# An order planned while the program is built, replaced by one written out in full (two H3 convolution and MLP layers)

## The chip, the cores and the metric

The kernel runs on one core of a Trainium2 chip. The metric is the device time of one execution in microseconds, lower is better. The engines are PE (TensorE, matrix products), DVE (VectorE), ACT (ScalarE), POOL (GpSimd) and SP (SyncE, which here only issues DMAs). Each engine takes its instructions in the order in which they stand in its own queue; an instruction that waits holds up those behind it.

## What is computed

```python
def _A_ref(q, k, v, shift_k, ssm_k, ssm_D):       # B=1, S=2048, D=512, 4 taps
    k_pad = jnp.pad(k, ((0, 0), (ks - 1, 0), (0, 0)))
    for t in range(ks):
        k_shift = k_shift + k_pad[:, t:t + S, :] * shift_k[:, ks - 1 - t][None, None, :]
    kv = k_shift * v
    ...                                            # y: causal convolution of kv with ssm_k
    y = y + kv * ssm_D[None, None, :]              # along S, per channel, by FFT of length 2S
    return q * y

def _B_ref(x, w1, b1, w2, b2):                     # 512 -> 1376 -> 512
    y = _layernorm(x, axis=-1)
    h = _gelu(jnp.einsum("bsd,df->bsf", y, w1) + b1)
    return jnp.einsum("bsf,fd->bsd", h, w2) + b2

x = A_q
x = x + _A_ref(_layernorm(x), A_k, A_v, A_shift_k, A_ssm_k, A_ssm_D)
x = x + _B_ref(_layernorm(x), B_w1, B_b1, B_w2, B_b2)
# the last two lines once more
```

All tensors are bf16. The convolution of `kv` does not depend on `x`, so the kernel computes `y` once and both layers use it.

## The kernel before

**The stages.** The program runs in two parts.

The first part makes `y`. The convolution is a product of spectra, and the transforms are matrix products. For the filter: transposes on PE (tag `ht`, L749), a first transform stage (`h1`, L766, 16 tiles), a second stage (`h2`, L779, 16 tiles), and 16 DMAs that store a copy of the spectrum with its two halves swapped. For `kv`: the four-tap shift of `k` and the product with `v` (tags `fir0` to `fir3`), where channels 0 to 255 go over PE (L810 transposes, L827 products with scaled identities that POOL makes at L741, L834 product with `v` on DVE) and channels 256 to 511 over DVE alone (L658, eight operations of 128x2048 for each 128 channels); then the first stage (`x1`, L766, 16 tiles), the second stage (`x2`, L872, 16 tiles) and the product with the filter's spectrum on DVE (L658, 16 operations), the first inverse stage (`i1`, L896, 16 tiles) and the second inverse stage (`i2`, L953, 10 tiles). The `x2`, `i1` and `i2` tiles come in two halves of the channels, `_0` and `_64`.

Every PE tile of this part goes to a pair of PSUM banks, and is then copied to SBUF by an evacuation, which can be on ACT (L663) or on DVE (L664); a tile whose bank pair is still in use waits for the evacuation of the tile before it there.

The second part runs the layers in blocks of rows (128 rows are a slice; layer 1 has blocks of 1, 1, 2, 2, 2, 2, 2, 2, 2 slices, layer 2 four of 4). Each block has statistics on DVE (L985, L987) with an inverse square root on POOL (L991, L993), a norm (tag `q`, L1000), the product with `y` and the sum into `x` (tag `y`, L658), the statistics and norm once more (tag `z`), and a transpose of the normed slice. That transpose is on PE for the first two slices (L1047) and a DMA on the SP queue for all others (L1039 in the code, two or four of them for a block). Then come the first product of the MLP (`m1`, L1060, 11 tiles of 4 matmuls for a block), GELU on ACT (L1065), the second product (`m2`, L1093, 11 matmuls for a slice) and its sum into `x` on DVE (L1097). The last slice of layer 2 has its second product in three pieces of 256, 128 and 128 columns (L1082, L1086). The results leave by DMAs of 128 or 256 KB, the last ones smaller. Blocks are named z0 to z8 (layer 1) and z19 to z22 (layer 2) after their tags.

**What sets the order.** The program is recorded first: each `P.op(...)` appends an operation with what it reads and writes, and `Prog` derives which earlier operations it depends on. Operations are numbered in the order of recording, 0 to 1113, and both kernels record the same ones under the same numbers. Then `schedule()` (L320 on) simulates the engines with assumed durations: at each step it picks, among the operations that are ready, the one of least start time and highest priority. The priority is the longest way to the end plus offsets from four tables (`BIAS` by tag, `PB` by operation, and delays `SHY`, `PS` and `HOLD`). It also picks the engine where two are allowed, unless the table `ENG` fixes it, and the PSUM banks, from pools: pairs of banks for the first part, and for the MLP one group of at most 3 banks for `m1` and one of at most 3 for `m2`. The engines' queues are the result. `sync()` then puts in the semaphore waits that the dependencies need, and `emit()` writes the instructions.

All loads and DMA transposes stand on the SP queue, but four small loads and one store that stand on ACT's. POOL's queue waits for its own instruction before, each time.

Of the kernel before, what the change touches and what calls it, by code (L numbers as in the profile page):

```python
# [7 lines left out]
ALU = mybir.AluOpType  # L8
# [14 lines left out]
class Pool:  # L23


    def __init__(self, nb, cap, gate=False):
        self.nb, self.cap, self.used, self.gate = nb, cap, 0, gate


class Tile:  # L30


    def __init__(self, pool):
        self.pool = pool
        self.base = None
        self.left = 0
        self.ops = []


class Op:  # L40
    __slots__ = ("i", "engs", "eng", "fn", "dur", "preds", "succ", "prio", "tile", "dma", "start", "end",
                 "pos", "inc", "waits", "val", "npred", "ready", "bytes", "base", "extra", "gate", "tag", "allow")


class Prog:
# [5 lines left out]
    LAT = 155.0  # L51
    BIAS = {'': 1044190, 'fir0': 816272, 'fir1': 594035, 'fir2': 1000293455, 'fir3': 475782, 'h1': 868926, 'h2': 42492, 'ht': 880650, 'i1_0': 1240071, 'i1_64':
        1212024, 'i2_0': 1097582, 'i2_64': 1190749, 'm1': 1032413, 'm2': -1808312, 'q0': 602778, 'q1': 1095651, 'q19': 267875, 'q2': 1096365, 'q20':
        912832, 'q21': 583017, 'q22': 318772, 'q3': 998981448, 'q4': 986060, 'q5': 466064, 'q6': 470208, 'q7': 409268, 'q8': 641212, 'taps': 736508,
        'warm0': 1000949769, 'x1_0': 1331587, 'x1_1': 783401, 'x1_2': 1063685, 'x1_3': 949292, 'x2_0': 377017, 'x2_64': 955361, 'y0': 1650539, 'y1':
        1623078, 'y19': 2204116, 'y2': 1000018107, 'y20': 947043, 'y21': 1812233, 'y22': 1073869, 'y3': 1411221, 'y4': 607830, 'y5': 295728, 'y6':
        405240, 'y7': 620020, 'y8': 1895488, 'z0': 999281074, 'z1': 1641796, 'z19': 1050878, 'z2': 131483, 'z20': -312548, 'z21': 457235, 'z22':
        577125, 'z3': -403715, 'z4': 81537, 'z5': 198870, 'z6': -330710, 'z7': 181103, 'z8': 1650154}
    SHY = {'fir0': 1021, 'fir1': 277, 'h1': 55, 'h2': 0, 'ht': 0, 'i1_0': 0, 'i1_64': 365, 'i2_0': 61, 'i2_64': 0, 'x1_0': 0, 'x1_1': 8, 'x1_2': 1351, 'x1_3':
        1268, 'x2_0': 0, 'x2_64': 462, 'z0': 261, 'z1': 833}  # L60
    PB = {0: 150814, 1: -52106, 2: -225577, 3: -123331, 4: 999221868, 9: 1276405, 44: 1379512, 45: 1434690, 47: 506509, 49: 453148, 51: 999588645, 52:
        1000042154, 53: 1589169, 54: 1589469, 55: 1517533, 56: 1595021, 57: 1561543, 58: 1589849, 59: 1505754, 60: 1589135, 61: 1539763, 63:
        999477473, 64: 999472326, 65: 81483, 66: 1000044663, 67: 999459987, 68: 19356, 69: 999454615, 70: 999472376, 71: -54290, 72: 999450473, 73:
        999474703, 75: 999467239, 76: -144374, 77: 999428971, 78: 239791, 79: 999491599, 80: 245756, 81: 999824582, 82: 168731, 83: 999955057, 84:
        -153184, 85: 1000209098, 86: 182551, 87: 999183272, 88: 316431, 89: 999956485, 90: -132325, 91: 999955107, 92: 228777, 93: 999458556, 94:
        -263977, 95: 1000286130, 96: -155038, 97: 999951289, 98: 491335, 99: 999392283, 100: 370445, 101: 999956535, 102: 370055, 103: 999943327, 104:
        316481, 105: 1000160828, 106: 1184366, 107: 1000314641, 108: 1291204, 109: 1000854551, 110: 1266991, 111: 1000849866, 112: 1230810, 113:
        1262509, 114: 1184316, 115: 745385, 116: 899745, 117: 1262559, 118: 909647, 119: 1001022447, 120: 893995, 121: 1000704463, 122: 834188, 123:
        874451, 124: 883372, 125: 1000706919, 126: 774582, 127: 998790820, 128: 785190, 129: 1000706969, 130: 861289, 131: 998997835, 132: 820442,
        133: 998980303, 134: 656521, 135: 998997885, 136: 907870, 137: 998958853, 155: -39187, 156: -120533, 157: -28284, 158: -97856, 159: 55705,  # L70
        161: -516310, 162: -336038, 163: -518892, 164: 205143, 165: 997729962, 166: -214054, 167: -532152, 169: 999878049, 170: 26055, 171: 341414,
        172: 302525, 173: -46374, 175: -516143, 176: -99172, 177: 431557, 178: -1035368, 179: 998060916, 180: -4231, 181: 998061019, 183: -127374,
        184: -999854529, 185: -1000132297, 186: -999488136, 187: -999485498, 188: -999373078, 189: -999483119, 191: 998075025, 192: -336655, 193:
        997785394, 194: -134666, 195: 998021352, 196: -685036, 197: 997910445, 199: -108657, 200: -207937, 201: 409421, 202: 73116, 203: -307100, 204:
        373599, 205: 669605, 207: 810393, 208: -569320, 209: 792122, 210: 501734, 211: 186163, 212: -176342, 213: 377429, 215: 1000696642, 216:
        998595356, 217: -50, 218: 1275751, 219: 756681, 220: -627082, 221: 998743003, 222: 555542, 223: 45, 224: 75226, 225: -102355, 226: 504322,
        227: 998924854, 228: 759137, 229: -343831, 230: 1363941, 231: 557998, 232: -624626, 233: 1513102, 234: 1001678, 235: 494654, 236: 998659113,
        237: 68724, 239: 639399, 240: -142796, 241: 322586, 242: 192764, 243: 740845, 244: 126297, 245: -566055, 246: 219170, 247: 608048, 248:
        -35318, 249: 380427, 250: 126247, 251: -1127529, 252: 103746, 253: 230758, 255: 998347921, 256: 998431917, 257: -11025, 258: 509829, 259:
        998025019, 260: 366769, 261: 998226716, 262: 998431967, 263: 31, 264: 703634, 265: 998431924, 266: 467759, 267: 922821, 268: 998451943, 269:  # L80
        412967, 270: 998227330, 271: 998451993, 272: 327804, 273: 742271, 274: 998037985, 275: 50337, 276: 999968359, 277: 998434335, 279: 298049,
        280: 152190, 281: 358015, 282: -341491, 283: 417985, 284: -1150, 285: 412598, 286: 226932, 287: -987359, 288: -107162, 289: 350905, 290:
        150350, 291: 634586, 292: -120566, 293: 998096146, 308: 1465845, 309: 1509084, 310: 1454263, 311: 1446566, 312: 1227621, 314: 524321, 315:
        31603, 316: 508933, 317: -181697, 318: 219814, 319: -282525, 320: 998097678, 321: -119423, 322: 485782, 324: 998069011, 325: -235296, 326:
        997992307, 327: -478329, 328: -1033996, 329: -376661, 330: -1029693, 331: -368979, 332: -703260, 334: 998659676, 335: 1899604, 336: 1936265,
        337: 493047, 339: 23181, 340: 997383373, 341: 997684387, 343: -246654, 344: 435848, 345: -996672795, 346: -996548852, 347: 406757, 348:
        -998727435, 349: 188797, 350: -772376, 351: -1657, 352: -560052, 353: 998190809, 354: -90796, 355: -101769, 356: -294390, 357: -22717, 358:
        -187974, 359: 817, 360: -210463, 361: -13499, 362: -297738, 363: 998339095, 364: -856719, 365: 46341, 366: -856722, 367: 47421, 368: -1031847,
        369: 387, 370: -465710, 371: -7105, 372: 1888330, 373: 1889303, 374: 2164277, 375: 2831282, 377: 998090342, 378: 1490839, 379: 1272509, 380:
        998131015, 382: 997525207, 383: 997659852, 384: 997906873, 386: -178, 387: 997432687, 388: 1099648, 389: 729514, 390: 998078479, 391: -667124,  # L90
        392: 997909179, 393: -90181, 395: -287849, 396: -1105208, 397: -643666, 398: 998193901, 399: -716417, 401: -716948, 402: -6378, 403: -1043716,
        404: 998714183, 405: -559050, 406: 998340752, 407: -668160, 408: 48098, 409: -735263, 410: -5564, 411: -296218, 412: 998197275, 413: -639571,
        414: 998616267, 415: 2069863, 416: 1900008, 417: 1873327, 418: 2950942, 420: 525435, 421: 997886742, 422: 526337, 423: 1432173, 424: 1606857,
        425: 597541, 427: -556199, 428: -385679, 429: -639224, 430: 998185257, 431: -467907, 432: -439130, 433: -560982, 434: -386814, 435: 999236624,
        436: 998821254, 437: 937285, 438: 999432304, 439: 999476812, 440: 999488740, 441: 2546841, 442: 2522318, 443: 998831934, 445: 1042685, 447:
# [166 lines left out]
    def op(self, eng, fn, dur, reads=(), writes=(), tile=None, dma=None, prio=0.0, nbytes=0, gate=()):  # L262
        o = Op()
# [10 lines left out]
        for t in o.tile:  # L274
            for p in t.ops:
                preds.add((p.i, "psum"))
# [857 lines left out]
```

## Time and profile before

| | |
|---|---|
| median of 3 runs | 241.92 us (241.72 to 242.06) |
| span of the profiled execution | 239.8 us |
| PE matmul busy | 226.5 us, 94% |
| PE weight loads | 151.5 us |
| DVE busy | 175.7 us, 73% |
| ACT busy | 142.9 us, 60% |
| POOL busy | 34.8 us |
| granted TensorE clock | 1.000 |
| HBM read, written | 16.82 MB, 2.10 MB |

The profiled execution's own time is its span of 239.8 us, from its first to its last instruction, and some 2.1 us around it that the runs' times contain and the span does not. The largest groups of instructions are:

| line, engine | what | count | busy us | mean ns |
|---|---|---|---|---|
| L1060 PE | first MLP product | 568 | 83.7 | 296 |
| L1093 PE | second MLP product | 329 | 78.9 | 379 |
| L663 ACT | evacuations | 79 | 73.9 | 1055 |
| L1065 ACT | GELU | 143 | 67.8 | 522 |
| L658 DVE | shift, spectral products, `y` | 108 | 63.8 | 628 |
| L985 DVE | statistics | 68 | 42.6 | 650 |
| L1000 DVE | norms | 64 | 24.1 | 401 |
| L1097 DVE | sums of the second product | 31 | 20.8 | 682 |

Means count overlap: a DVE or ACT instruction starts before the one ahead of it is done, so its cost on a full engine is the distance from start to start, which is some 0.1 us less than the mean of the large ones. The same holds for matmuls.

### The profile page before, as it was taken

How to read it: one execution, taken by the hardware profiler on the slowest of the kernel's cores; microseconds unless marked ns; L12 is line 12 of the kernel's file. 1: busy time of each engine (PE TensorE's matmuls, PEld its weight loads, DVE VectorE, ACT ScalarE, POOL GpSimd, SP SyncE). 2: the span in 40 equal slices, each digit the busy share in tenths (PEclk: the TensorE clock that was granted, in tenths of full speed). 3: DMA queues.
4: the chain of work that ended last, by engine and by line, in shares of the span. 5: the costliest groups of instructions: out<-in, count | busy, mean ns of one | idle time of the engine just before them, and what ended most of it. 6: DMA issues, size and time to landing. Idle time of an engine off the chain costs nothing.

```text
span 239.8 us, 5559 instructions
## 1 busy us (share of the span) xinstructions
PE 226.5 (94%) x2310; PEld 151.5 (63%) x2330; DVE 175.7 (73%) x363; ACT 142.9 (60%) x223; POOL 34.8 (15%) x75
## 2 busy tenths in 40 slices
PE   7988899886899999999999999999999999999996
PEld 3876777775899885777767665754444444444453
DVE  0779999999997989989999996978997401211214
ACT  3697999999998994665556253464532552436200
POOL 3250000000012222223141032022130100000000
PEclk9999999999999999999999999999999999999999
DMA  6999999999910004222020203313022203210022
GB/s 231 338 387 385 384 235 272 249 282 337 375 63 0 3 0 48 45 44 48 0 44 5 42 1 68 66 23 68 0 44 44 87 3 69 62 44 0 3 98 77
DMA packets 37035, 27.40 MB, mean 114 GB/s; under 512 B 19506, under 2 KB 29969, under 8 KB 37010
## 3 DMA queue, kind: packets, MB, share of 16 engines
q1 hardware_dynamic: 36446, 26.91, 38.1%
q8 instruction: 18, 0.29, 0.5%
q10 hardware_dynamic: 564, 0.14, 0.4%
q14 instruction: 7, 0.06, 0.1%
HBM read 16.82 MB, written 2.10 MB: 79 GB/s over the span
## 4 chain that ended last, share of the span: by engine, by line
PE 71%; DVE 15%; DMA 4%; ACT 4%; SPq 3%; issue 2%; DVEq 0%
PE ps L1060 32%; PE ps L1093 30%; DVE ar L658 8%; PE ps L896 5%; DMA ar<-in_A_v_dram 4%; ACT ar L663 4%; DVE ar L664 4%; SPq L647 3%; DVE ar L834 2%; PE ps L1082 1%; PE ps L872 1%; DVE sm L985 1%; PE ps L953 1%; DVE ar L1000 0%; PE ps L766 0%
## 5 line engine op out<-in xcount | busy, mean ns | idle before, releaser
L1065 ACT ACTIVATE ar<-ps,sm 128x256 bf16<-128x256 f32 (+5 forms) x143 | 67.8, 522 | 72.8 <-PE ps L1060 70.1
L1060 PE MATMUL ps<-ar 128*128 128x256 bf16 (+5 forms) x568 | 83.7, 296 | 0.2
L1093 PE MATMUL ps<-ar 128*128 128x512 bf16 (+1 forms) x329 | 78.9, 379 | 0.7
L663 ACT ACTIVATE ar<-ps 128x1024 bf16<-128x1024 f32 (+2 forms) x79 | 73.9, 1055 | 8.0 <-PE ps L766 3.2
L1060 PEld LDWEIGHTS ps<-ar 128*128 128x128 bf16 (+1 forms) x572 | 53.2, 100 | 29.4 <-ACT ar L1065 0.4
L658 DVE TENSOR_TENSOR ar<-ar 128x512 bf16<-128x512 bf16 (+3 forms) x108 | 63.8, 628 | 1.8 <-DMA ar<-in_A_k_dram 1.4
L1093 PEld LDWEIGHTS ps<-ar 128*128 128x128 bf16 (+1 forms) x341 | 33.2, 98 | 34.5
L1097 DVE TENSOR_TENSOR ar<-ar,ps 128x512 bf16<-128x512 bf16 x31 | 20.8, 682 | 43.2 <-PE ps L1093 43.1
L985 DVE BATCH_NORM_STATS2 sm<-ar 128x6 f32<-128x512 bf16 (+1 forms) x68 | 42.6, 650 | 0.3
L1000 DVE TENSOR_SCALAR ar<-ar,sm 128x512 bf16<-128x512 bf16 x64 | 24.1, 401 | 6.6 <-POOL sm L993 6.3
L993 POOL TENSOR_TENSOR sm<-sm 128x2 f32<-128x2 f32 (+2 forms) x26 | 20.5, 787 | 2.2
L766 PE MATMUL ps<-ar 128*64 128x128 bf16 x512 | 17.6, 221 | 3.0 <-DVE ar L664 1.0
L991 POOL TENSOR_SCALAR sm<-sm 128x2 f32<-128x2 f32 (+2 forms) x26 | 5.9, 226 | 95.9 <-DVE sm L987 95.7
L766 PEld LDWEIGHTS ps<-ar 128*64 128x64 bf16 x512 | 14.9, 110 | 5.4 <-DVE ar L664 1.3
L664 DVE CAST ar<-ps 128x1024 bf16<-128x1024 f32 (+1 forms) x15 | 17.5, 1181 | 0.4 <-PE ps L872 0.2
L896 PE MATMUL ps<-ar 128*128 128x128 bf16 x256 | 15.1, 220 | 1.0 <-DVE ar L658 0.5
L896 PEld LDWEIGHTS ps<-ar 128*128 128x128 bf16 x256 | 14.5, 114 | 1.4 <-ACT ar L663 0.8
L872 PE MATMUL ps<-ar 128*128 128x64 bf16 x256 | 9.6, 193 | 2.3 <-ACT ar L663 2.1
L664 DVE COPY ar<-ps 128x2048 bf16<-128x2048 bf16 (+1 forms) x6 | 5.7, 954 | 7.6 <-PE ps L749 7.4
L987 DVE BATCH_NORM_AGGREGATE sm<-sm 128x2 f32<-128x6 f32 (+1 forms) x64 | 10.8, 177 | 0.6
L872 PEld LDWEIGHTS ps<-ar 128*128 128x128 bf16 x256 | 8.2, 98 | 3.5 <-ACT ar L663 3.4
L779 PE MATMUL ps<-ar 128*128 128x128 bf16 x128 | 8.7, 220 | 0.9 <-ACT ar L663 0.8
(33 smaller groups left out, 72.0 us busy)
## 6 DMA issues: line engine op xcount, KB each, us to landing
ar<-tab_s SPq DMA_DIRECT2D x16, 256.0 KB, 10.0
ar<-ar SPq DMA_DIRECT2D x16, 256.0 KB, 4.6
ar<-in_A_ssm_k_dram SPq DMA_DIRECT2D x4, 512.0 KB, 5.5
ar<-in_A_k_dram SPq DMA_DIRECT2D x8, 256.0 KB, 7.7
ar<-in_A_v_dram SPq DMA_DIRECT2D x8, 256.0 KB, 9.7
ar<-in_A_q_dram SPq DMA_DIRECT2D x4, 512.0 KB, 7.8
out_dram<-ar SPq DMA_DIRECT2D x7, 256.0 KB, 2.0
ar<-in_B_w_dram SPq DMA_DIRECT2D x1, 1376.0 KB, 12.0
```

The source lines that it names most:

```text
L658: return P.op(eng, lambda e: e.tensor_tensor(o, a, b, op), dur, reads=[a, b] + list(more), writes=[o])
L663: return e.activation(dst, src(), AF.Copy)
L664: return e.tensor_copy(dst, src())
L766: r = e.matmul(Q(tl, 64 * ri, 64, i * 128, [1, 128]), w, m, start=True, stop=True)
L896: r = e.matmul(Q(tl, 0, 128, i * 128, [1, 128]), w, m, start=q == 0, stop=q == 1)
L985: P.op(DVE, lambda e, sj=sj, x=x: e.bn_stats(sj, x), 40.0 + 1.1 * w, reads=[x], writes=[sj], gate=gate)
L993: P.op(POOL, lambda e: e.tensor_tensor(r, v, hf, ALU.pow), 430.0 + 150.0 * n, reads=[v, hf], writes=[r])
L1000: P.op(DVE, lambda e: e.tensor_scalar(o, x, m, r, ALU.subtract, ALU.mult), 335.0, reads=[x, m, r], writes=[o])
L1060: r = e.matmul(Q(tl, 0, rows, 0, [1, w]), a, m, start=dk == 0, stop=dk == 3)
L1065: P.op(ACT, lambda e, dst=dst, tl=tl, rows=rows, bias=bias, w=w: e.activation(dst, Q(tl, 0, rows, 0, [1, w]), AF.Gelu_apprx_tanh, bias=bia ...
L1093: r = e.matmul(Q(tl, 0, 128, 0, [1, 512]), ins[fc][0], ins[fc][1], start=fc == 0, stop=fc == 10)
L1097: P.op(DVE, lambda e, x=x, tl=tl: e.tensor_tensor(x, x, Q(tl, 0, 128, 0, [1, 512]), ALU.add), 640.0, reads=[x], writes=[x], tile=tl)
```

## The change

`schedule()`, its tables and the pools go. In their place stand three tables: `ORDER`, one permutation of the numbers 0 to 1113; `SECOND`, the operations that run on the second of their two allowed engines; and `BANKS`, the first PSUM bank of each tile in the order of recording. `arrange()` reads them. The queue of an engine is the subsequence of `ORDER` whose operations are its own. `sync()` and `emit()` stay, but that waits are sorted by place in `ORDER` instead of by simulated end.

```diff
-        self.banks = [(0.0, []) for _ in range(8)]
-        free = {e: 0.0 for e in (PE, ACT, DVE, POOL, SP)}
...
-            k = (s + (self.PS.get(o.i, self.SHY.get(o.tag, 300.0)) if e == DVE and len(o.engs) > 1 and o.dur[DVE] > o.dur.get(ACT, 1e9) else 0.0), -o.prio, o.i)
...
+    def arrange(self):
+        self.order = {e: [] for e in (PE, ACT, DVE, POOL, SP)}
+        last = [None] * 8
+        second = set(self.SECOND)
+        assert sorted(self.ORDER) == list(range(len(self.ops)))
+        for at, i in enumerate(self.ORDER):
+            o = self.ops[i]
+            o.eng = o.engs[i in second]
+            o.at, o.pos = at, len(self.order[o.eng])
+            self.order[o.eng].append(o)
+            tl = o.tile
+            if tl is not None and tl.base is None:
+                tl.base = self.BANKS[tl.i]
+                for b in range(tl.base, tl.base + tl.nb):
+                    if last[b] is not None:
+                        for p in [p for p in last[b].ops if p.eng != PE] or last[b].ops[-1:]:
+                            assert p.eng is not None
+                            if p.i not in o.preds:
+                                o.preds[p.i] = "psum"
+                    last[b] = tl
...
-                    cands.sort(key=lambda x: -x.end)
+                    cands.sort(key=lambda x: -x.at)
...
-            tl = Tile(dconv)
+            tl = Tile(2)
```

`Tile(2)` is a pair of banks, `Tile(1)` a single one (MLP products and the PE transposes of z0 and z1). The tables begin so:

```python
ORDER = (
    0, 47, 8, 7, 48, 5, 3, 71, 68, 72, 73, 6, 1, 62, 98, 104, 16, 2, 69, 4, 65, 15, 63, 70, 64, 53, 102, 11, 13, 32, 49, 57, 99, 66,
    105, 100, 101, 80, 103, 50, 81, 17, 67, 76, 74, 56, 9, 51, 90, 52, 77, 94, 91, 96, 75, 19, 14, 12, 36, 95, 44, 18, 25, 27, 78, 60,
...
SECOND = (
    63, 64, 66, 67, 69, 70, 72, 77, 85, 89, 91, 97, 101, 161, 179, 191, 197, 213, 251, 283, 324, 392)
BANKS = (
    0, 2, 0, 2, 2, 0, 4, 0, 4, 6, 0, 2, 2, 6, 6, 4, 2, 0, 4, 4, 0, 6, 4, 6, 0, 6, 2, 6, 0, 4, 6, 4, 4, 6, 4, 2, 2, 0, 0, 2, 0, 4, 6, 2,
...
```

Put side by side, the two programs differ in this:

- The operations are the same 1114. PE has 343 of them in both, SP 109; ACT has 230 instead of 228, DVE 358 instead of 363, POOL 74 instead of 71.
- 31 operations change engine. From ACT to DVE: one copy of the transposed filter (66), six `h1` evacuations (77, 85, 89, 91, 97, 101), three `x1` (179, 191, 213), two `i1` (251, 283), one `i2` (324). From DVE to ACT: three `h1` (79, 87, 99), three `h2` (113, 117, 123), the copy of the transposed `k` of channels 0 to 127 (155), two `x1` (175, 211), one `x2` (224), three `i1` (249, 285, 293), one `i2` (314), the copy of the transposed slice z0 (349). From DVE to POOL: three additions of `ssm_D` to one row of the filter (64, 67, 70).
- The loads on SP stand in another order: the four filter loads as 8, 7, 5, 6; then `k`, `v` and the 16 loads of the second-stage table mixed, instead of `k`, `v`, table. Each halo load of `k` stands among them (11 early, 10 behind the last of `k`). The swapped copies of the filter's spectrum (138 to 153), the loads of the inverse table (294 to 297), of `A_q` (298 to 301) and of the weights (302 to 307) are mixed too.
- Of the `i2` tiles, 313 now stands before the last four `i1` tiles on PE, and 321 behind the transpose of z0. z0 is transposed before z1, where it was z1 before z0.
- Statistics and norms of later blocks stand earlier on DVE, in part by several blocks. In layer 1, the first two-slice block starts on PE (451) before the second products of the one-slice blocks are done (374, 416, 417 follow).
- On PE the last tile is the 256-column piece of the last slice (1105); it was a 128-column piece (1111).
- 513 of the 624 operations that use a PSUM tile use other banks than before. The number of semaphore waits falls from 976 to 854.

## The prediction

> **What bounds the kernel now.** I read the 40 slices first, then the chain of waits, then the timelines of DVE and ACT, then busy time by stretch.
>
> ```profile
> PE   7988899886899999999999999999999999999996
> DVE  0779999999997989989999996978997401211214
> ACT  3697999999998994665556253464532552436200
> ```
>
> PE is full from about 64 us to the end. Before that DVE and ACT are full (slices 4 to 12), and PE is not. The chain shows the same change of hands:
>
> ```profile
> 63.52 1.13 ACT ar L663
> 64.70 3.84 PE ps L896 x64
> 68.53 0.09 issue
> 68.63 8.21 PE ps L896 x144
> 76.83 0.45 PE ps L953 x4
> 77.31 0.70 DVE ar L664
> 82.61 0.34 DVE ar L1000
> 83.00 0.40 PE ps L1047 x4
> ```
>
> From 64.70 PE works without a gap but at two places: 76.83 to 83.00, where it runs the second inverse stage (L953) level with DVE's first layernorms, and 94.27, where the block after the two one-tile blocks starts 0.04 us after its transposed input landed (94.23).
>
> ```profile
> 200.00:210.00 10.00, 9.95 (x47) 4.50 (x46) 1.97 (x3) 2.74 (x5) 0.00 (x0) 1.00 0.32 74
> 210.00:220.00 10.00, 9.95 (x47) 4.65 (x47) 0.75 (x2) 5.38 (x8) 0.00 (x0) 1.00 0.07 26
> ```
>
> Columns: window, then PE, weight loads, DVE, ACT, POOL, granted clock. PE is at 9.95 of 10 at clock 1.00, and four 128x512 matmuls take 0.86 us, 2.4 columns a ns. Since no matmul is added or removed, the time can only fall by PE idling less before 95 us. So I follow one thing: when PE reaches a given piece of its work. [...]
>
> **The change, part by part.** What fills DVE and ACT:
>
> ```profile
> 16.80 2.36 DVE L658 TENSOR_TENSOR ar<-ar 128x2048 bf16<-128x2048 bf16 x2 [1.43 <-DMA ar<-in_A_k_dram]
> 50.23 18.25 DVE L658 TENSOR_TENSOR ar<-ar 128x2048 bf16<-128x2048 bf16 x16
> 52.62 20.27 ACT L663 ACTIVATE ar<-ps 128x1024 bf16<-128x1024 f32 x22 [0.23 <-DVE ar L658]
> ```
>
> One large DVE operation costs 1.136 us ((18.25-1.21)/15), one ACT evacuation 0.92 (20.27/22; starts are 0.905 apart).
>
> 1. Engines. 13 evacuations go ACT to DVE, 15 DVE to ACT, three 1x128 additions DVE to POOL. DVE's work falls by two evacuations and 0.66 us, about 2.1 us with the small ones (172.2 to 170.1, summed from its row durations); ACT's rises about 1. What matters is where: six of the 16 stage-1 evacuations of the filter and all four of the transposed filter now stand on DVE ahead of the convolution; before it was three and three. Before 16.80, while DVE waits for k (1.43 us), it has done 6 large operations; now it has 9 queued ahead.
>
> 2. Loads. The SP queue lands 256 KB every 0.67 us in order. Two table loads now stand ahead of k's last part and the 0.78 us halo behind it: k lands at 16.78+2x0.67-0.78 = 17.3 instead of 16.78. DVE's nine: first transposed tile at 6.2, 9x1.136+0.2 = 10.4 of work, and about 1.4 of waits, mostly for the fourth filter load (9.73 plus 1.2 of transposes, where DVE was free at 10.1): 18.0. So k's delay is covered by 0.7, and would cost what exceeds that.
>
> 3. Up to the products. Then 25 large DVE operations stand before the first spectral product, 28.4 us: 46.4. Before it was 29 from 16.80, 50.23 with 0.5 idle. ACT agrees: its first stage-1 tile is ready at 9.5 (transposes in step 2, then 0.66 on PE), and ten such evacuations at 0.905, two tap copies of 0.5 and two copies of the transposed k of 1.87 end at 23.3, with small waits 23.5; 24 more at 0.905 bring the first product's tile at 45.2, in SBUF at 46.2; before it was started at 49.53. The 0.43 us of PE per stage-1 tile hides under these. SP's swaps of the filter's halves wait for ACT's evacuation at about 35; the fourth lands near 43, covered by 3; the table loads behind them are first needed at 73.
>
> 4. Products and first inverse. On DVE 17 large operations and one 0.60 bn_stats: 19.9, so the last product ends at 66.5 with 0.2 of waits; before 68.48. PE starts the second half's tiles at 66.95 (before 68.60) and runs eight at 0.89 plus one 0.44 tile of the second inverse, moved between them: 74.5. Before, it ended its last such tile at 76.6 without the 0.44. PE is ahead by 76.6+0.4-74.5 = 2.5.
>
> 5. First layernorms. The moved 0.44 tile and its evacuation on ACT (0.55) let y start at 74.1 instead of 78.03. DVE's queue from there has 5.3 of work to the first z norm and 0.4 of wait: 79.8. PE, with 5.7 of second-inverse tiles after 74.5, transposes that z at 80.3 (before the first at 82.99, with 0.3 lost): ahead by 2.7. Evacuations of the last inverse tiles now sit between ACT's GELUs of the one-tile blocks, 0.26 each: one makes PE wait about 0.15.
>
> 6. Transposed inputs. PE's order puts the first two-tile block 2.2 us of work earlier: ten matmuls of the second MLP product, 0.216 each, now follow its start. From the first z transpose it has 8.8 of work to there (two transposes of 0.22, 0.87 of second inverse, the 22 tiles of the first MLP product at 0.222, 12 matmuls at 0.216), and the gap of 0.3 that it also showed before: 80.3+8.8+0.3 = 89.4. DVE's norms end at 85.2, the two transposes are issued one after the other (1.27 each) and the second lands 2.5 after its issue: 88.8. Before the second took 3.86 (90.37 to 94.23); if that recurs, 90.1, and PE waits 0.7. Counting blocks from z0, I did the same for the later ones: DVE's queue up to the block's last norm, plus its idle so far, plus 3.4 to landing (as for z4 and z5 before), against PE's queue up to the block's first matmul. PE finds each landed, by 0.6 (z3), 0.7 (z5), 1.0 and 0.8 (first two of layer 2) and by over 1 elsewhere; before, this margin was 1.7 to 4 after z2. DVE's longer waits for second-product tiles come behind the norms that are near.
>
> 7. Tail. The last PE tile is 256 wide, not 128: DVE 0.42 for 0.29, landing 1.53 for 1.46: 0.2 lost.
>
> 8. Banks: any of eight instead of two groups of three for the MLP. PE waits for none of them before; the cover is a freed bank 0.7 us ahead, and gone it would cost that wait per block. Nothing, 0 to 0.7.
>
> The three additions on POOL are the one price the trace lacks. Nearest rows: POOL's 128x1 tensor_tensor 0.57, its 128x128 scale 0.61, so 1.2 to 1.8 for three; they delay the eight scaled identities to 18.9, needed by PE at 21.7. Nothing, 0 to 0.3. DVE's 1x128 additions took 0.43 for two while POOL scaled, 0.22 alone, so no stretch. [...]
>
> Sum: 2.7, less 0.2 for ACT, 0.2 for half a late landing and small waits, 0.2 tail: 2.1. Profiled span 239.8, and 2.1 outside it to the median of 241.92; 237.7 + 2.1 = 239.8. Unknowns give 1.2 worse (0.7 landing or banks, 0.3 POOL, 0.2) to 1.1 better (no early waits, 0.9 of the 1.4, and 0.2): 238.7 to 241.0.
>
> **The rivals.**
> - Half of it: the late landing recurs (0.5 more than charged) and bank or POOL waits take 0.5: 240.8. For it: 3.86 was seen once; against: every other pair took 2.4 to 2.6.
> - No change: the early stage is bound by hand-overs. Stage-1 tiles take PE 0.43 start to start but 0.66 start to ready, and in the new order nearly each waits for a bank just freed. With 0.6 instead of 0.43 over some 12 tiles in series the first product comes 2.0 later, 48.5, and the gain is 0.1: 241.8. Against it: before, DVE kept 84% busy through the same stage.
> - Slower: one DVE stall becomes PE's. In the new queue DVE has 30.8 us of work between the first z norm and z5's last norm (before 22.6), since statistics of later blocks are drawn forward. Without idle PE has 0.7 to spare there. Before, DVE idled 3.7 in that stretch (POOL's 0.87 twice among it). If it idles so again, z5's block is 3.0 late, and PE, in order, waits: 239.8+3.0 = 242.8. It decides from 2.8 of idle. Against: the drawn-forward work fills those waits; I find only one of 0.35.
>
> **How the numbers follow.** Forecast 0.52, half 0.20, no change 0.12, slower 0.16. What a measurement can tell is 0.2%, 0.5 us: faster 0.72, same 0.12, slower 0.16. The forecast's own range is 238.7 to 241.0; the range reaches on to 242.4, leaving out most of the slower case and a little below.
>
> **What would show it.** First product on DVE near 46.4; k's wait gone; last product near 66.5; first z transpose on PE near 80.3; the first two-tile block near 89.4; PE then at 9.9 of 10. A first product after 48, or PE idle at a block start above 0.7, proves a step wrong.

## The result, and the profile after

| | before | after |
|---|---|---|
| median, us | 241.95 (241.72 to 242.06, 4 runs) | 244.57 (242.91 to 245.59, 4 runs) |
| ratio after to before | | 1.0103, 95% interval 1.006 to 1.0147 |
| span of the profiled execution, us | 239.8 | 241.1 |
| PE matmul, DVE, ACT busy, us | 226.5, 175.7, 142.9 | 228.3, 172.7, 140.0 |

The changed kernel is 1.0% slower; 239.8 was forecast. The profiled execution after is the fastest of its four (242.91). One execution of the changed kernel in the first experiment below took 598.18 us, and that experiment's figures leave it out.

The slices and the queue of PE's instructions, from the page of the changed kernel:

```profile
PE   6996999887899999999999999999999999999995
DVE  0799699999999999999699789968772532100133
ACT  2397999999999995446426524703584013638000
...
q8 instruction: 18, 0.29, 0.5%
```

As before, PE is full from slice 12 on (66 us); DVE has a 6 in its fifth slice (24 to 30 us), where it had a 9. The stretch that PE bounds has not become shorter or longer (columns as before: window, PE, weight loads, DVE, ACT, POOL, granted clock, DMA share, GB/s):

```profile
200.00:210.00 10.00, 10.00 (x48) 4.51 (x47) 2.06 (x3) 5.46 (x9) 0.00 (x0) 1.00 0.08 28
```

So the loss must stand at the front. The chain of waits after:

```profile
19.62 1.11 PE ps L589 x18
20.74 2.28 issue
23.02 0.94 PE ps L589 x14
23.96 0.89 PE ps L558 x16
24.85 1.76 PE ps L606 x14
26.61 0.02 issue
26.63 1.23 DVE ar L613
...
66.05 8.35 PE ps L674 x144
74.40 0.44 PE ps L731 x4
```

In the middle of one PE tile (op 154, sixteen transposes) PE does nothing for 2.28 us, and "issue" says that it waited for nothing that the profile shows. Behind two further tiles (114 and 120) stands the product that DVE needs (op 172). The timeline of DVE after shows what that costs:

```profile
21.09 3.48 DVE L450 TENSOR_TENSOR ar<-ar 128x2048 bf16<-128x2048 bf16 x3
26.63 1.23 DVE L613 TENSOR_TENSOR ar<-ps,ar 128x1024 bf16<-128x1024 f32 x1 [2.05 <-PE ps L606]
...
49.74 2.35 DVE L450 TENSOR_TENSOR ar<-ar 128x2048 bf16<-128x2048 bf16 x2
...
62.02 8.21 DVE L450 TENSOR_TENSOR ar<-ar 128x2048 bf16<-128x2048 bf16 x7
```

DVE waits 2.05 us before op 173, which takes that product, and is full from there to the last spectral product (70.22). The milestones, from the traces (at the two ends of its last stretch PE is read by its weight loads):

| us | before | predicted | after |
|---|---|---|---|
| first tap operation, DVE | 16.80 | 18.0 | 18.82 |
| first spectral product, DVE | 50.23 | 46.4 | 49.74 |
| last spectral product ends | 68.48 | 66.5 | 70.22 |
| first z transpose, PE (its first weight load) | 82.99 | 80.3 | 83.84 |
| from there to the end of PE's last weight load | 154.31 | | 154.37 |
| from that end to the end of the span | 2.46 | | 2.91 |

### The profile page after: what moved, and what is told of

The parts are those of the page before. It is cut to its first block, busy times and chain, and to the rows that moved or that the text cites. A ratio compares the mean times of both kernels' runs of the same rounds, so it can differ in the third digit from the quotient of the medians.

```text
span 241.1 us, 5575 instructions
## 1 busy us (share of the span) xinstructions
PE 228.3 (95%) x2330; PEld 152.5 (63%) x2330; DVE 172.7 (72%) x358; ACT 140.0 (58%) x225; POOL 37.6 (16%) x78
## 4 chain that ended last, share of the span: by engine, by line
PE 79%; DVE 8%; ACT 8%; DMA 2%; issue 2%; DVEq 0%
PE ps L827 32%; PE ps L860 31%; ACT ar L453 8%; DVE ar L450 5%; PE ps L674 5%; PE ps L731 3%; PE ps L528 2%; PE ps L545 2%; DVE ar L613 2%; DMA ar<-in_A_ssm_k_dram 2%; PE ps L651 2%; PE ps L849 1%; DVE ar L453 1%; PE ps L589 1%; PE ps L606 1%
## 5 line engine op out<-in xcount | busy, mean ns | idle before, releaser
L832 ACT ACTIVATE ar<-ps,sm 128x256 bf16<-128x256 f32 (+5 forms) x143 | 64.2, 523 | 71.3 <-PE ps L827 58.1
L827 PE MATMUL ps<-ar 128*128 128x256 bf16 (+5 forms) x572 | 82.6, 297 | 0.1
L860 PE MATMUL ps<-ar 128*128 128x512 bf16 (+1 forms) x341 | 79.9, 379 | 0.0
L453 ACT ACTIVATE ar<-ps 128x1024 bf16<-128x1024 f32 (+3 forms) x81 | 74.7, 1059 | 8.4 <-PE ps L545 6.5
L768 DVE TENSOR_SCALAR ar<-ar,sm 128x512 bf16<-128x512 bf16 x64 | 24.9, 409 | 5.9 <-POOL sm L762 3.1
L453 DVE CAST ar<-ps 128x1024 bf16<-128x1024 f32 (+1 forms) x14 | 16.3, 1180 | 0.5 <-PE ps L545 0.2
L674 PE MATMUL ps<-ar 128*128 128x128 bf16 x256 | 15.0, 220 | 0.6 <-ACT ar L453 0.6
L853 DVE TENSOR_TENSOR ar<-ar,ps 128x128 bf16<-128x128 bf16 (+1 forms) x3 | 0.9, 330 | 14.0 <-PE ps L849 14.0
L453 DVE COPY ar<-ps 128x2048 bf16<-128x2048 bf16 (+1 forms) x5 | 5.2, 1062 | 7.8 <-PE ps L528 7.8
L756 DVE BATCH_NORM_AGGREGATE sm<-sm 128x2 f32<-128x6 f32 (+1 forms) x64 | 10.2, 172 | 0.4
```

The costliest lines, as they stand in the source:

```text
L453: f = {ACT: lambda e: e.activation(dst, src(), AF.Copy), DVE: lambda e: e.tensor_copy(dst, src())}
L674: r = e.matmul(Q(tl, 0, 128, i * 128, [1, 128]), w, m, start=q == 0, stop=q == 1)
L768: P.op(DVE, lambda e: e.tensor_scalar(o, x, m, r, ALU.subtract, ALU.mult), reads=[x, m, r], writes=[o])
L827: r = e.matmul(Q(tl, 0, rows, 0, [1, w]), a, m, start=dk == 0, stop=dk == 3)
L832: P.op(ACT, lambda e, dst=dst, tl=tl, rows=rows, bias=bias, w=w: e.activation(dst, Q(tl, 0, rows, 0, [1, w]), AF.Gelu_apprx_tanh, bias=bia ...
L860: r = e.matmul(Q(tl, 0, 128, 0, [1, 512]), ins[fc][0], ins[fc][1], start=fc == 0, stop=fc == 10)
```

## The experiments

Three theories stand against each other. F: PE's next instructions come late. H: PE loses its time in hand-overs with the evacuations (the prediction's "no change"). C: PE runs its first transposes slowly (0.107 us from one to the next in the changed kernel until 8.25 us, 0.062 after; the expectations call this half rate). What speaks for F is in the transfers of the changed kernel between 15.6 and 20.5 us, and between 20.5 and 21.7 (queue and kind, packets, MB, share of 16 engines):

```profile
q1 hardware_dynamic: 1205, 1.72, 106.6%
...
q1 hardware_dynamic: 244, 0.44, 100.3%
q8 instruction: 1, 0.02, 5.8%
```

One packet of 16 KB goes over queue 8 in the second window (start 20.54, took 1.11 us), and none in the 4.9 us before, while loads fill all engines. 18 such packets run in the program; the last eight (from 82 us on, with the DMA engines under 50% busy in each slice) start 256 recorded PE instructions apart in the mean (251 in the kernel before). That they carry PE's instructions, the author inferred from the queue's kind and this distance. PE stood behind its 693rd recorded instruction; it was 256 instructions back at 15.6 us, which is the estimate from which the first window starts.

**The changed kernel again.**

> The changed kernel as it is, for its spread and a second profile. Theory F (PE's code comes late: in the profiled run PE stood from 20.74 to 23.02 us in the middle of 16 transposes, waiting for nothing the profile shows, while an instruction fetch of 16 KB ran from 20.54 to 21.65 among loads that kept the DMA engines full): runs spread over more than 1 us, 242.5 to 246, and the profile has one gap on PE of 2 us or more at the same instruction, whatever its length. Theory H (hand-overs between PE and the evacuations, the prediction's third rival): runs within 0.5 us of each other, as those of the kernel before, and no such gap.

243.83 us in the median of five, from 243.37 to 245.49; ratio 1.0094 (1.0066 to 1.0122). The gap is there: 21.05 to 23.26, behind the same 693 recorded instructions of PE as in the first profile. F as expected, and H cannot explain a place fixed in the program.

**Fewer loads outstanding** (`held` lists the first 38 loads on SP).

```diff
+        for a, b in zip(held, held[5:]):
+            self.ops[b].preds[a] = "held"
```

> The changed kernel, but each of the first 38 loads on SP waits until the load five places ahead of it has landed, so that five transfers are outstanding instead of some fifteen. Order and sizes of all loads stay. Theory F: the fetch gets through sooner, the gap of 2.28 us on PE goes, DVE's wait of 2.05 us at 24.6 falls below 0.3, the last spectral product ends near 68.3 instead of 70.22, the time falls by 1.5 to 3 us to 241 to 242, and its runs agree within 0.5. Theory H: gap and wait stay, the time is the same or, by later loads, longer.

The mechanism came, the gain did not. The fetch starts at 18.30, no gap is left in op 154, and op 173 starts at 25.55 instead of 26.88 in the run beside it. But the loads fall from 358 to 279 GB/s between 10 and 20 us, table loads come late (PE waits 2.41 for one at 25.96), and the time is 245.24. So the edit was too broad, and narrower ones follow. The first line is hold1's, the second hold27's; each has this one instead of the lines above.

```diff
-        self.ops[25].preds[14] = "held"
+        self.ops[27].preds[14] = "held"
```

> The changed kernel with one wait added: the sixteenth load on SP (256 KB of v) waits until the twelfth (256 KB of k, landed at 15.56 us) is in, so that only three loads are outstanding when PE comes to the place, at about 15.6, from which its fetch took 5 us to start. Loads behind it land in the same order. Theory F: the fetch starts near 18 instead of 20.5, PE's gap of 2.2 to 2.4 us at 20.7 goes (0 to 0.4 left), 154 ends near 21.4 instead of 23.8, DVE's op 173 starts at 24.6 to 25.0 instead of 26.63, the last product ends near 68.5, the time falls by 1.5 to 3 us to 241.3 to 242.3, with no run at a granted clock of 0.993. The rival, that five outstanding loads cost held5 its gain in bandwidth and that the gap is not what sets the time: gap gone, but last product still at 70 and the time at 243.5 to 244.5.

> As hold1, with the wait one load later (the seventeenth load waits for the twelfth), so that four loads instead of three are outstanding at 15.6 us. In hold1 the gap in op 154 went, but the loads then paused (226 GB/s at 14 to 18 us, 374 in the changed kernel) and PE waited 1.14 us for a table load at 22. Theory F: the fetch starts at 18.5 to 19.5, at most 0.5 us of gap is left, the pause of the loads is shorter, op 173 starts at 24.6 to 25.2 (25.53 in hold1), time 242.0 to 242.9. If the length of the queue does not decide, the gap is back at 2 us and the time at 244.

hold1: 242.99, ratio 1.0054 (1.0028 to 1.0079), between what F and its rival expected. hold27: 242.07, ratio 1.0018 (0.9995 to 1.0042), in the range that F expected and level with the kernel before, though in its profile op 173 starts at 26.08, not at 24.6 to 25.2. PE in hold1, timeline:

```profile
19.41 2.13 PE L590 MATMUL ps<-ar 128*128 128x128 bf16 x32
21.37 0.61 PE L559 MATMUL ps<-ar 128*128 128x128 bf16 x8
23.13 0.62 PE L559 MATMUL ps<-ar 128*128 128x128 bf16 x8 [1.15 <-DMA ar<-tab_s]
23.59 1.91 PE L607 MATMUL ps<-ar 128*128 128x512 bf16 x14
```

The 32 transposes run through, where the changed kernel has "x18", a gap and "x14". What is left is a wait for a load, which the hold made late; in hold27 it is 0.63 us of the gap instead. By the ratios, one wait on one load takes 1.0 us (hold1) and 1.8 us (hold27) off, and PE's gap goes or shrinks as its fetch starts sooner: F is shown. In hold27's profile luck had a part: PE came to the place at 21.84, 1.10 us later than in the changed kernel's (20.74), and went on 0.55 us sooner. Over the profiles, with the start of the fetch that PE needs at this place:

| kernel | fetch starts | PE goes on | difference | gap |
|---|---|---|---|---|
| after, again | 20.54, 20.79 | 23.02, 23.26 | 2.48, 2.47 | 2.28, 2.21 |
| warm8, taps, tail128 | 20.72, 21.59, 21.58 | 23.13, 24.07, 23.99 | 2.41, 2.48, 2.41 | 2.39, 2.03, 2.30 |
| hold27, fix2, both | 19.87, 19.40, 20.41 | 22.47, 21.84, 23.06 | 2.60, 2.44, 2.65 | 0.63, 1.09, 1.49 |
| held5, hold1, fix4, fix5 | 18.30, 18.23, 17.74, 16.57 | | | none in this tile |

From the packet's start to PE's next instruction it takes 2.41 to 2.65 us, whether the gap is 0.63 or 2.39. In the kernel before the fetch started as late, at 20.56. PE's timeline there, and its instruction queue between 20.5 and 21.7:

```profile
20.35 0.64 PE L766 MATMUL ps<-ar 128*64 128x128 bf16 x16 [0.97 <-DVE ar L664]
21.15 1.69 PE L827 MATMUL ps<-ar 128*128 128x384 bf16 x13 [0.16 <-issue]
22.77 0.76 PE L766 MATMUL ps<-ar 128*64 128x128 bf16 x16
...
q8 instruction: 1, 0.02, 5.8%
```

PE had issued 642 recorded instructions when the packet started, 693 after: it had waited 0.97 us for an evacuation, and stood next before a tile of long matmuls (1.85 us for 28 instructions). It came to its 693rd at 23.0; 2.41 to 2.65 us from the packet's start end at 22.97 to 23.21. The older order hid the fetch behind a wait and long matmuls that it had anyway.

**The start of PE.**

```diff
-        for i in range(6):
+        for i in range(8):
```

> The changed kernel with 8 instead of 6 warm-up matmuls of 512 columns on PE ahead of everything, so that PE is busy until about 4.9 us instead of 4.05, when the first filter load lands; before, the two matmuls of the taps stood there. Theory C (PE started at half rate: its first 48 transposes came 0.095 us apart in the mean, 0.072 before, because it was idle for 0.79 us): the first 32 transposes take about 2.3 us instead of 3.3, the first evacuation starts on DVE near 6.4 instead of 6.81, the nine evacuations end near 18.2 instead of 18.9, the time falls by 0.6. Theory F: the gap moves forward by two transposes, since four instructions were added, PE still goes on at about 23.0, and the time stays within 0.3.

244.14, ratio 1.0082 (1.0051 to 1.0112): no gain. The transposes change from 0.106 to 0.06 us at 7.17 us, sooner than in the seven profiles with six warm-ups and the taps late (8.25 to 10.74), but the first tap operation starts at 18.94, no sooner than in the changed kernel's (18.82). As F expects, the gap moved by the four instructions added, to behind 16 transposes instead of 18. The trace names an evacuation on ACT as what PE waits for there, since the next tile begins at that place; it had ended at 19.97, and the gap begins at 20.74. And this profile shows a stretch at a lower clock behind the gap (windows of warm8):

```profile
22.00:24.00 2.00, 0.87 (x16) 0.87 (x16) 2.00 (x3) 0.66 (x1) 0.00 (x0) 1.00 1.05 386
24.00:26.00 2.00, 2.00 (x22) 1.73 (x20) 0.82 (x1) 1.78 (x2) 0.00 (x0) 0.56 1.05 387
26.00:28.00 2.00, 2.00 (x12) 1.19 (x11) 0.00 (x0) 1.93 (x3) 0.00 (x0) 0.59 1.05 383
```

The third number from the end is the granted clock: 0.56 and 0.59 from 24 to 28 us; the gap ended at 23.13. The fourteen matmuls of 512 columns that DVE waits for then take 2.96 us (1.91 in the changed kernel's profile), and DVE waits 3.69 instead of 2.05.

```diff
-    0, 47, 8, 7, 48, 5, 3, 71, ...
+    0, 1, 3, 47, 8, 7, 48, 49, 50, 5, 71, ...
```

> The changed kernel with one part undone: the two matmuls of the taps and their two copies on ACT stand where they stood before, behind the warm-up and ahead of the transposes (with the load that they need, and on banks of their own). Theory C: PE is at its full rate from the first or second tile of transposes in most runs (0.06 to 0.07 us from one to the next instead of 0.106), the evacuations ahead of the first tap operation end at 18.0 to 18.3 instead of 18.8 to 19.8. Theory F: PE then only stands longer at the same instruction, until about 23, so that op 173 still starts at 26.3 to 26.9 and the time falls by 0 to 0.4. If C is the main cause, op 173 starts at 25.8 and the time falls by 0.8 or more.

243.71, ratio 1.0078 (1.0048 to 1.0107), not to be told from the changed kernel. The load that the taps need landed at 4.8, so the transposes started at 5.78 instead of 4.84 and were no faster. The median does not show C as a price, nor refute it. The ten profiles with the taps late do show that the first tap operation follows the change of rate: it starts at 18.32 to 18.94 where that comes at 5.99 to 7.17 (eight warm-ups: fix5, fix4, warm8), at 18.73 to 19.13 where it comes at 8.25 to 9.12, and at 19.67 to 19.92 where it comes at 9.23 to 10.74.

**The tail.**

```diff
-    ..., 1105, 1099, 1106, 1107)
+    ..., 1111, 1099, 1112, 1113)
```

> The changed kernel with the 256-column and the second 128-column piece of the last slice exchanged in the order and in their banks, so that the last PE tile is 128 wide, as before. From the end of PE's last tile to the end of the span it took 2.9 us, before 2.5. If the tail is worth what the prediction said, the time falls by 0.2, by the traces by 0.4; theory F expects all else to stay, the gap on PE too, and its scatter may hide the 0.2 to 0.4.

244.00, ratio 1.0081 (1.0062 to 1.0101): within the scatter. From the end of PE's last weight load to the end of the span it takes 3.13 us, not less than 2.91. DVE in tail128:

```profile
239.28 0.69 DVE L868 TENSOR_TENSOR ar<-ar,ps 128x512 bf16<-128x512 bf16 x1 [1.20 <-PE ps L864]
239.90 0.29 DVE L857 TENSOR_TENSOR ar<-ar,ps 128x128 bf16<-128x128 bf16 x1
```

The small sum stands right behind a 512-wide one, but starts only 0.04 us after PE's last matmul (239.86), so it is hardly held up itself. What is held up is its transfer: the 256 KB behind the 512-wide sum are issued at 239.99 and the last 32 KB at 240.37, and the packets of both run together until 241.79, 1.61 us after the last sum's end. In the kernel before, the last 512-wide sum starts 1.23 us before the last small one; there the last transfer ran alone and ended 1.14 us after its sum. So the tail costs more than the width of its last piece; moving the 512-wide sum was not tried.

**Put together.** both is hold1 and taps, all3 adds tail128.

> hold1 and taps together. Theory F with C: gap gone and first transposes faster, op 173 at 24.0 to 24.5, first product at 47.0 to 47.5, last product near 67.6, time 240.5 to 241.3, which is below the kernel before (241.97). If something else holds the first stage (theory H, hand-overs), the first product stays at 49 or later.

> both, and the last two pieces of the last slice exchanged as in tail128, which itself took 0.3 from the median. Expected 240.2 to 241.0, and runs within 0.7 of each other; by theory H 243 or more.

242.71 (1.0029 to 1.0057) and 242.99 (1.0036 to 1.0076): no better than hold1, and 1.4 and 2.0 above the upper end of what was expected. In the kernel both, the fetch came at 20.41 in spite of the hold, and 1.49 us of the gap was left; in all3 it came at 19.51 and none was left, but there the first tap operation started at 20.16, since the taps again held up the transposes. How far a hold helps goes with the landing of the load that it waits for: where that was at 15.4 to 15.6 (hold1, fix4, fix5) the fetch started at 16.6 to 18.2, where it was at 13.9 to 14.0 (hold27, fix2, both, all3) at 19.4 to 20.4.

fix2 is hold27 with op 172 ahead of op 120 on PE; fix4 adds warm8 and tail128.

> hold27, and on PE the product with the tap matrices that DVE waits for (op 172) ahead of a second-stage tile (op 120) whose table load comes late. Theory F: the rest of DVE's wait ahead of op 173 goes, 173 starts at 24.3 to 24.8, the first product at 47.4 to 47.9, the last near 68.3, the first z transpose on PE at 81.9 to 82.4, and since from there to PE's end it took 154.4 us in every run, also in the kernel before, the time is 241.3 to 242.2, level with the kernel before (241.8). Theory H: no change against hold27.

> fix2 with 8 warm-up matmuls (warm8) and the 128-column piece last (tail128). Theory C: PE reaches its full rate 1 to 2 us sooner (7.2 in warm8, 8.3 to 9.3 in the others), the first tap operation on DVE starts at 18.0 to 18.5, worth 0.2 to 0.6, the tail 0.3: 240.6 to 241.6. If the cold start is worth nothing, 241.2 to 241.9.

242.73 (1.0004 to 1.0038) and 242.49 (1.0002 to 1.0037): as hold27 or slightly above, and 0.5 to 0.6 above the ranges expected. The profile of fix2 has a wait that belongs to none of the theories. The profile of the unchanged order (again) has it too, in DVE's timeline:

```profile
62.27 3.48 DVE L450 TENSOR_TENSOR ar<-ar 128x2048 bf16<-128x2048 bf16 x3
66.50 4.63 DVE L450 TENSOR_TENSOR ar<-ar 128x2048 bf16<-128x2048 bf16 x4 [0.75 <-DMA ar<-ar]
```

A spectral product (277) waits for a swapped copy of the filter's spectrum (152). It could start at 43.5, but stands on SP behind seven loads (three of the input, one of the inverse table, three of weights and biases), and lands at 63.7 to 67.6 us over the profiles; before, the last swap landed at 52.4. The order on SP at this place, in the changed kernel and in fix5:

```diff
-    306, 298, 296, 153, 304, 305, 299, 151, 150, 300, 152
+    153, 151, 150, 152, 298, 306, 296, 304, 305, 299, 300
```

> hold27 with 8 warm-up matmuls, and on SP the last four swapped copies of the filter's spectrum (150 to 153, which could start at 43.5 us) ahead of the loads of the input and the weights that stand between them. In hold27, fix2, again and tail128 the product 277 on DVE waited 0.4 to 0.75 us for swap 152, which landed at 64.9 to 67; with the exchange it lands near 58 and that wait is gone, so that from the first to the last product it takes 20.5 us as in the changed kernel. Theory F with this: time 241.2 to 241.9, that is 0.2 to 0.5 below hold27 (242.07) or fix4 (242.49). If the late swaps do not matter, the same as these, 242.0 to 242.6.

241.65, ratio 0.9987 (0.9974 to 1.0): as expected, 0.4 below hold27, and a little below the kernel before, at the edge of what can be told. That is 0.3 us of the 2.1 that were forecast. The swap lands at 57.67, and DVE runs through (fix5):

```profile
61.71 8.21 DVE L455 TENSOR_TENSOR ar<-ar 128x2048 bf16<-128x2048 bf16 x7
```

Its profile is its slowest run (242.62), with PE waits of 1.01 and 1.88 us for table loads at 21.5 and 25.3: the hold still costs. That fix5 owes its gain to the swaps and not to the warm-ups was not separated.

## Why the prediction was wrong

The predicted span was 237.7; it was 241.1. The 3.4 us lie, by the prediction's own steps:

| step | predicted | measured | us |
|---|---|---|---|
| 2: nine evacuations done, first tap operation | 18.0 | 18.82 | +0.8 |
| 3: 25 large operations on DVE, without a wait | 28.4 | 30.92 | +2.05 waiting for PE, +0.5 |
| 4: first to last product | 20.1 | 20.48 | +0.4 |
| 4, 5: from there to the first z transpose | 13.8 | 13.62 | -0.2 |
| 6, 7: from there to the end | 157.4 | 157.28 | -0.1 |

**Step 3 failed.** It said that PE's time per tile "hides under" DVE and ACT, and let DVE run 25 operations without a wait. PE was taken as ready whenever data and bank were. Its instructions were not, for 2.28 us, so that the first product came at 49.74 instead of 46.4, 2.05 us of it by this wait; and the hold, which moves only loads, gave 1.0 us (hold1) to 1.8 us (hold27) back. The page of before showed 18 instruction packets and a full DMA through that time; the prediction asked for neither. It costed the order of the loads by when each lands, not by how many stand ahead of a fetch.

**Step 2 was off in size.** The last large piece of k landed at 17.42 (predicted 17.3), and DVE did not wait for it. The first transposed tile reached DVE at 6.81 instead of 6.2, because the transposes came slower; the nine evacuations and their waits took the rest. In the timelines of PE, before and after:

```profile
4.97 2.44 PE L749 MATMUL ps<-ar 128*128 128x128 bf16 x32
```

```profile
4.84 4.56 PE L528 MATMUL ps<-ar 128*128 128x128 bf16 x48 [0.80 <-DMA ar<-in_A_ssm_k_dram]
```

0.076 against 0.095 us each. Since the taps no longer stand there, PE idles from 4.05 to 4.84. The prediction moved those matmuls without counting them. In the changed kernel the transposes follow each other at 0.107 us until 8.25 and at 0.062 after; in the kernel before between waits for loads, they come at 0.062 from the second one (5.08) on. Over the ten profiles with the taps late, the change comes at 5.99 to 10.74; what sets its time was not shown. The profiles put the price at some 0.3 us of the first tap operation for each us of delay (18.32 at 5.99, 19.92 at 10.74); no run isolates what it costs in all.

**The median** lies 1.7 above the profiled run. Two of the four runs had a granted clock of 0.993 and are the two slowest (245.35, 245.59). There is no profile of them; warm8's, at 0.992, puts the lost clock behind the gap. But hold1, hold27 and fix4 also had one run each at 0.993 (245.43, 244.52, 243.99), which hold1's expectation excluded; that the gap brings these runs about is not shown. None of the 82 runs of the kernel before beside the experiments was under 0.999.

**What held.** From the first z transpose on nothing was won or lost (154.37 against 154.31), so neither banks nor drawn-forward statistics cost anything in this profile. The scaled identities came at 20.43 instead of 18.9 and were needed at 24.63, so POOL's additions were covered. One price on POOL is in no term of the forecast's sum. The last identity, in POOL's timeline after:

```profile
18.78 1.64 POOL L520 TENSOR_SCALAR ar<-ar,sm 128x128 bf16<-128x128 bf16 x1
```

The other seven took 0.60 or 0.61. This one met DVE's first tap operation (18.82, 1.22 us as ever), and POOL lost 1.04 us, DVE nothing. It took 1.50 to 1.65 us in the eleven profiles in which the two start within 0.2 us of each other and POOL is at most 0.04 us ahead; where it was 0.10 us ahead (warm8) it took 0.60 and DVE's operation 1.34. The traces show these times, not what makes them. None of this delayed the products on PE. The swaps on SP, "covered by 3", were right for the first four only: the last one had 0.5 us left in this profile, and DVE waited 0.26 to 0.75 us for it in five others.

**The rivals.** The slower case has the sign but not the mechanism: its stall on DVE before block z5 is in no profile (again shows 0.74 us of PE waiting for a transposed input at 171.8, once). "No change" put the first product at 48.5 for a PE too slow between tiles; it came at 49.74 for one stall. No rival was about instructions arriving, and the range ended at 242.4 because every term in it was data, banks or engines.

## What to carry to other kernels

PE ran out of instructions here in the middle of short ones (18 transposes in 1.18 us) while loads filled the DMA engines (106.6%, 100.3%): it stood 2.0 to 2.4 us in five profiles. In a kernel like it, count the instructions to the next instruction packet, and ask what is queued ahead of it; an order that takes out waits can lose them again there. One well-placed wait on a load may then be worth more than the full rate of the loads, as in hold27 (ratio 1.0018 against 1.0094 without it); a wait on each of 33 loads (held5, 1.0141) cost more than it gave. And when copies and loads share a queue, look at the last copy's landing (here 63.7 to 67.6 us, before 52.4), not the first one's.

## What was not expected of the hardware

- From the start of PE's 16 KB packet to its next instruction it takes 2.41 to 2.65 us, in eight profiles. While loads ran at 340 to 390 GB/s the packet started at 20.5 to 21.6; with the loads held back, at 16.6 to 20.4, although PE had come as far at the same time (18.25 and 18.16 for the same tile in the changed kernel and hold1).
- The last scaled identity on POOL took 1.50 to 1.65 us instead of 0.60 where it met DVE's first tap operation, in eleven profiles.
- A gap of 2.39 us on PE, ended at 23.13, was followed by a granted clock of 0.56 to 0.59 from 24 to 28 us in one profile; in four others, with gaps of 2.0 to 2.3, by no such stretch.
- At 15.6 us 14 loads of another queue are outstanding in the changed kernel, three by its edit in hold1; the packet starts at 20.54 and 18.23. Why it comes later with more of them stays open.
